# Decode attention with a gated FFN: every large load issued as two halves of 64 partitions, from SyncE's queue and from ScalarE's

## The chip, the core and the metric

The kernel runs on one core of a Trainium2 chip. The metric is the device time of one execution in microseconds. All inputs lie in HBM and have to be brought into SBUF, the on-chip memory with 128 partitions. Five engines work side by side, each through its own queue in program order: TensorE (PE in the profile, PEld for its weight loads), VectorE (DVE), ScalarE (ACT), GpSimd (POOL) and SyncE (SP). DMAs are issued by an engine's queue and carried out by 16 DMA engines, which the profile shows together as DMA.

## The reference

One decode step for a batch of 4 with 32 heads of 128, a cache of 4096 keys and values for each head, and a GEGLU feed-forward layer beside it. All data are float32.

```python
q = (x @ wq).reshape(4, 1, 32, 128).transpose(0, 2, 1, 3)
p = softmax(einsum("bhqd,bhkd->bhqk", q, k_cache) * 128 ** -0.5)
a = einsum("bhqk,bhkd->bhqd", p, v_cache)      # transposed and reshaped to (4, 1, 4096)
a = a @ wo
b = (gelu(x @ w_gate) * (x @ w_up)) @ w_down
g = sigmoid((x * gate_w).sum(-1, keepdims=True))
out = g * a + (1 - g) * b
```

The key cache and the value cache are 268 MB each, so nearly all the bytes are k and v, and each is used once.

## The kernel before

The work is cut into NT = 64 steps. Step i takes two heads (a pair of heads, g = i // 4) of one batch element (b = i % 4). For each step there is one k load and one v load, each a tile `kv` of 128 partitions by 8192 float32 (32 KB in each partition, 4 MB in all): 64 partitions belong to each of the two heads, and a partition holds 64 rows of the cache. The pool `kv` has five such buffers. The query weights wq (two tiles), the FFN's w_gate and w_up (one tile each) and w_down (one tile, filled by four DMAs) pass through the same five buffers.

All loads come from one list, in the order in which they are needed: q0, q1, k0, k1, v0, k2, v1, k3, v2, and so on. The function `load` (L51) issues one entry, and `load_next` takes the next entry of the list. The last v tile, v63, is loaded in two DMAs that split its columns. The output weights wo come in 16 loads of 512 KB into a pool of their own (`load_wo`, L87 to L89), one every four steps, and gate_w in 13 tiny ones (`load_gw`). All DMAs are issued by SyncE.

In the main loop, step i does this, in this program order:

- `scores_a(i)` (L187): VectorE multiplies the last 8 of the 64 cache rows in each partition with the query (tile `pa`).
- `soft_max(i - 1)`: VectorE takes the maximum per head (L214, the second `m`), TensorE spreads it to the partitions (L217), ScalarE scales it (L219, `nb`) and takes the exponentials (L222, `pm`).
- `scores_d(i)`: four times VectorE multiplies 14 rows (L187, `pr`) and sums them (L198); ScalarE sums the 8 rows of `pa` (L200). Then comes one `load_next`.
- `pv(i - 1)` (L247): TensorE multiplies the probabilities with the v tile, in 32 matmuls. Then comes another `load_next`.
- `o_out(i - 1)`: ScalarE copies the result out of PSUM (L254, `o`), TensorE folds it with 8 passes (L258, `oT`).
- `max_a(i)`: VectorE takes the maximum of a partition (L207), TensorE transposes it (L209).

After step 1 the two `load_next` of step i issue v(i+1) and k(i+3). A load into a `kv` buffer has to wait until the buffer's last reader is done: the last product of VectorE for a k tile, the last matmul of `pv` for a v tile. `q_spread` (L175, L178, tile `qb`) prepares the queries of the next pair of heads every four steps, `project_a` and `ffn_down` (both by L240) are the output products, and after step 63 there is one more pass (i = 64) with `pv(63)`, the last projections, and the result's DMA (L363).

The Tile framework adds the waits. It gives every DMA, whichever engine issues it, one of eight completion semaphores in turn. A DMA that is given a semaphore again waits until the DMA that had it before, eight DMAs earlier, has landed. That wait stands on the queue of the issuing engine, ahead of the DMA, and everything behind it on that queue waits too.

Of the kernel before, what the change touches and what calls it, by code (L numbers as in the profile page):

```python
# [17 lines left out]
def tile_gated_mix(ctx: ExitStack, tc: tile.TileContext, x, kc, vc, wq, wo, w_gate, w_up, w_down, gate_w, out):  # L18
    nc = tc.nc
    P = 128  # L20
    B, H, S, D = kc.shape
    DM = x.shape[2]
    F = w_gate.shape[1]
    KC = DM // P
# [6 lines left out]
    TW = R * D  # L31
# [16 lines left out]

    T = {}

    def load(kind, i):  # L51
        t = T[kind, i] = kv.tile([P, TW], F32, name="kv")
        if kind in "kv":
            h, b = HT * (i // B), i % B
            src = (kc if kind == "k" else vc)[b, h:h + HT].rearrange("h (p r) d -> (h p) (r d)", p=PH)
            n = 2 if (kind, i) == ("v", NT - 1) else 1
            for s in range(n):
                nc.sync.dma_start(t[:, s * TW // n:(s + 1) * TW // n], src[:, s * TW // n:(s + 1) * TW // n])  # L58
        elif kind == "q":
            nc.sync.dma_start(t, wq.rearrange("(p c) n -> p (c n)", c=KC)[:, i * TW:(i + 1) * TW])  # L60
        elif kind == "f":
            nc.sync.dma_start(t[:, :KC * F], (w_gate, w_up)[i].rearrange("(p c) n -> p (c n)", c=KC))
        else:
            for f0 in range(0, F, FG):
                f1 = min(f0 + FG, F)
                n = (f1 - f0) // P
                nc.sync.dma_start(t[:, f0 // P * DM:(f0 // P + n) * DM],
                                  w_down[f0:f1].rearrange("(p i) n -> p (i n)", i=n))

    loads = [("q", 0), ("q", 1), ("k", 0)]  # L70
    for i in range(NT):
# [8 lines left out]
    def load_next():  # L80
        n = next(loads, None)
        if n:
            load(*n)
# [302 lines left out]
```

## Time and profile before

| what | value |
|---|---|
| median of 3 runs | 1329.67 us (1329.47 to 1330.52) |
| the profiled execution | 1329.66 us |
| its span, from the first to the last instruction | 1327.9 us |
| TensorE's mean granted clock | 0.653 |
| busy: VectorE, TensorE, ScalarE | 1147.5, 536.3, 325.7 us |
| read from HBM | 564.67 MB, 425 GB/s over the span |
| k loads, v loads: median from issue to landing | 42.6 us, 34.2 us |

The 1.76 us between the profiled execution's own time and its span lie outside of the recorded instructions. An issue-to-landing time is not the time that a transfer needs by itself: it holds the wait behind the transfers that were issued earlier. The share of DMA is counted over all 16 DMA engines.

### The profile page before, as it was taken

What the parts mean: (1) busy time and instruction counts of PE and PEld (TensorE: products, weight loads), DVE (VectorE), ACT (ScalarE), POOL (GpSimd) and SP (SyncE); (2) the same over time, 40 slices, a digit from 0 to 9 for tenths busy, and PEclk for the clock granted to TensorE, in tenths of its full rate; (3) what the DMA queues carried; (4) which work ended last, traced back from release to release, by engine and by line L of the source; (5) the groups of instructions that cost most, each with busy time, mean ns of one, the idle gap of its engine ahead of it and who ended that gap; (6) DMA issues with size and microseconds to landing.
All of it is one profiled execution on the core that took longest, in us unless ns stands there. A gap on an engine that the chain in (4) does not pass through costs nothing.

```text
span 1327.9 us, 10223 instructions
## 1 busy us (share of the span) xinstructions
PE 536.3 (40%) x3690; PEld 191.2 (14%) x3690; DVE 1147.5 (86%) x783; ACT 325.7 (25%) x1435; POOL 0.7 (0%) x6
## 2 busy tenths in 40 slices
PE   3243433443442453443443343343343344343345
PEld 1011111111120121111111111111111111111112
DVE  1999898898898679889889889889889889889885
ACT  0232222223222122312312212212312312212211
POOL 0000000000000000000000000000000000000000
PEclk9656666666666775665666676666666666665677
DMA  9999999999999999999999999999999999999996
GB/s 411 426 425 434 432 427 426 436 427 429 429 433 429 428 430 431 430 430 430 430 429 432 430 427 433 431 429 426 431 433 430 429 427 436 427 427 433 431 428 287
DMA packets 24414, 565.33 MB, mean 426 GB/s; under 512 B 2712, under 2 KB 2728, under 8 KB 6956
## 3 DMA queue, kind: packets, MB, share of 16 engines
q1 hardware_dynamic: 24364, 564.69, 99.3%
q8 instruction: 29, 0.48, 0.1%
q14 instruction: 21, 0.17, 0.0%
HBM read 564.67 MB, written 0.01 MB: 425 GB/s over the span
## 4 chain that ended last, share of the span: by engine, by line
DMA 68%; DVE 26%; PE 4%; issue 1%; SPq 0%; ACT 0%; DVEq 0%; ACTq 0%
DMA kv<-in_A_k_cache 50%; DMA kv<-in_A_v_cache 18%; DVE pr L187 13%; DVE sc L198 11%; PE po L247 4%; DVE pa L187 2%; PE q L289 0%; DVE m L214 0%; PE b_acc L240 0%; SPq L58 0%; DVE m L207 0%; PE oT L258 0%; ACT pm L222 0%; DVE ot L270 0%; SPq L60 0%
## 5 line engine op out<-in xcount | busy, mean ns | idle before, releaser
L247 PE MATMUL po<-kv,pm 128*8 128x512 f32 x2048 | 364.8, 878 | 490.4 <-DMA kv<-in_A_v_cache 488.0
L198 DVE TENSOR_REDUCE sc<-pr 128x14 f32<-128x1792 f32 x256 | 517.1, 2020 | 8.8
L187 DVE TENSOR_TENSOR pr<-kv,qb 128x1792 f32<-128x1792 f32 x256 | 516.9, 2019 | 6.6
L254 ACT ACTIVATE o<-po 128x512 f32<-128x512 f32 x64 | 38.2, 597 | 584.1 <-PE po L247 584.1
L247 PEld LDWEIGHTS po<-kv,pm 128*8 128x8 f32 x2048 | 67.2, 116 | 736.8 <-issue 725.7
L187 DVE TENSOR_TENSOR pa<-kv,qb 128x1024 f32<-128x1024 f32 x64 | 78.4, 1224 | 107.8 <-DMA kv<-in_A_k_cache 107.8
L200 ACT ACTIVATE dump<-pa 128x128 f32<-128x128 f32 x512 | 158.3, 309 | 18.8 <-DVE pa L187 3.2
L200 ACT ACTIVATION_READ_ACCUMULATOR dump<-pa 128x1 f32 x512 | 95.3, 186 | 0.0
L258 PE MATMUL oT<-sel,o 128*128 128x2 f32 x512 | 67.4, 254 | 45.5 <-ACT o L254 45.5
L217 PE MATMUL sm<-m,ones 1*64 1x1 f32 x256 | 23.1, 244 | 154.3 <-DVE m L214 154.3
L219 ACT ACTIVATE nb<-sm 128x1 f32<-128x1 f32 x64 | 11.0, 171 | 295.9 <-PE sm L217 295.8
L258 PEld LDWEIGHTS oT<-sel,o 128*128 128x128 f32 x512 | 61.9, 191 | 107.1 <-ACT o L254 107.1
L209 PE MATMUL sm<-ident,m 128*1 128x128 f32 x64 | 18.6, 290 | 76.1 <-DVE m L207 75.5
L222 ACT ACTIVATE pm<-sc,nb 64x64 f32<-64x64 f32 x128 | 44.9, 351 | 2.8
L217 PEld LDWEIGHTS sm<-m,ones 1*64 1x64 f32 x256 | 17.7, 190 | 170.5 <-DVE m L214 169.3
L222 ACT ACTIVATION_READ_ACCUMULATOR pm<-sc,nb 64x1 f32 x128 | 23.7, 185 | 0.0
L178 ACT ACTIVATE qb<-q 128x512 f32<-128x512 f32 x16 | 9.6, 597 | 51.7 <-PE q L175 51.7
L175 PE MATMUL q<-ident,QT 128*64 128x128 f32 x256 | 20.1, 306 | 0.6 <-DVE QT L162 0.6
L207 DVE TENSOR_REDUCE m<-sc 128x1 f32<-128x64 f32 x64 | 14.1, 220 | 6.6
L214 DVE TENSOR_REDUCE m<-sm 1x2 f32<-1x128 f32 x64 | 17.3, 270 | 0.5 <-PE sm L209 0.5
L240 PE MATMUL a_acc<-wo_sb,ot 128*32 128x128 f32 x256 | 16.9, 412 | 0.0
L209 PEld LDWEIGHTS sm<-ident,m 128*1 128x1 f32 x64 | 5.1, 80 | 79.5 <-issue 38.3
(49 smaller groups left out, 95.0 us busy)
## 6 DMA issues: line engine op xcount, KB each, us to landing
kv<-in_A_k_cache SPq DMA_DIRECT2D x64, 4096.0 KB, 42.6
kv<-in_A_v_cache SPq DMA_DIRECT2D x63, 4096.0 KB, 34.2
kv<-in_A_wq SPq DMA_DIRECT2D x2, 4096.0 KB
wo_sb<-in_A_wo SPq DMA_DIRECT2D x16, 512.0 KB, 43.1
kv<-in_A_v_cache SPq DMA_DIRECT2D x2, 2048.0 KB
kv<-in_B_w_gate SPq DMA_DIRECT2D x1, 3584.0 KB
kv<-in_B_w_up SPq DMA_DIRECT2D x1, 3584.0 KB
kv<-in_B_w_down SPq DMA_DIRECT2D x3, 1024.0 KB, 26.4
```

Of the source, the lines that this page charges most:

```text
L175: nc.tensor.matmul(ps[h * PH:(h + 1) * PH, b, :], QT[:, HT * g + h, b:b + 1].to_broadcast([P, PH]), ident, start=True, stop=True)
L187: nc.vector.tensor_tensor(t, k[:, r0:r1], QB[g][:, b:b + 1, :].to_broadcast([P, r1 - r0, D]), op=OP.mult)
L198: nc.vector.tensor_reduce(SC[i][:, r0:r1], pr, axis=AX.X, op=OP.add)
L200: nc.scalar.activation(dump, PA[i][:, r - A_ROWS[0], :], AF.Copy, accum_out=SC[i][:, r:r + 1])
L209: nc.tensor.transpose(MT[i], m1, ident)
L214: nc.vector.tensor_reduce(m2, MT[i].rearrange("o (h p) -> o h p", h=HT), axis=AX.X, op=OP.max)
L217: nc.tensor.matmul(nbp[h * PH:(h + 1) * PH, :], ones[:1, :PH], m2[:, h:h + 1], start=True, stop=True)
L222: nc.scalar.activation(PM[i % 3][s, :, h], SC[i][s, :], AF.Exp, bias=nb[s, :], scale=scale, accum_out=RS[g % 2][s, b, h:h + 1])
L240: nc.tensor.matmul(acc[32 * c:32 * c + 32, :], t, w[:, c * C4:(c + 1) * C4], start=start, stop=stop)
L247: nc.tensor.matmul(PO[i % 2][32 * c:32 * c + M].rearrange("p j d -> p (j d)"), p[:, j * M:(j + 1) * M], T["v", i][:, j * N:(j + 1) * N], s ...
L254: nc.scalar.activation(o, PO[i % 2], AF.Copy)
L258: nc.tensor.matmul(OT[g][:, b, :], o[:, j, :], sel[:, j, :], start=j == 0, stop=j == RJ - 1)
```

## The change

A helper `rows` issues each large load twice: partitions 0 to 63 from SyncE's queue, partitions 64 to 127 from ScalarE's. It stands in for every `dma_start` in `load`, so for wq, k, v, w_gate, w_up and w_down; the two column halves of v63 and the four parts of w_down are each split in the same way, which makes 137 DMAs into 274. The loads of x, wo and gate_w and the store of the result stay whole on SyncE's queue. Bytes, buffers and arithmetic are the same.

```diff
+    def rows(dst, src):
+        for eng, p in ((nc.sync, 0), (nc.scalar, P // 2)):
+            eng.dma_start(dst[p:p + P // 2], src[p:p + P // 2])
+
     def load(kind, i):
...
             for s in range(n):
-                nc.sync.dma_start(t[:, s * TW // n:(s + 1) * TW // n], src[:, s * TW // n:(s + 1) * TW // n])
+                rows(t[:, s * TW // n:(s + 1) * TW // n], src[:, s * TW // n:(s + 1) * TW // n])
         elif kind == "q":
-            nc.sync.dma_start(t, wq.rearrange("(p c) n -> p (c n)", c=KC)[:, i * TW:(i + 1) * TW])
+            rows(t, wq.rearrange("(p c) n -> p (c n)", c=KC)[:, i * TW:(i + 1) * TW])
         elif kind == "f":
-            nc.sync.dma_start(t[:, :KC * F], (w_gate, w_up)[i].rearrange("(p c) n -> p (c n)", c=KC))
+            rows(t[:, :KC * F], (w_gate, w_up)[i].rearrange("(p c) n -> p (c n)", c=KC))
         else:
...
-                nc.sync.dma_start(t[:, f0 // P * DM:(f0 // P + n) * DM],
-                                  w_down[f0:f1].rearrange("(p i) n -> p (i n)", i=n))
+                rows(t[:, f0 // P * DM:(f0 // P + n) * DM], w_down[f0:f1].rearrange("(p i) n -> p (i n)", i=n))
```

In the program as built, ScalarE's queue has in step i, in this order: the 8 sums of `pa` (L200 of before), ScalarE's half of v(i+1), its half of k(i+3), then the copy `o` of step i - 1. In step 62 the four halves of w_down stand there, ahead of the copy `o` of step 61. With twice the DMAs in the same eight semaphores, the DMA eight before is only about two steps back: k(i+3) waits for a half of k(i+1) in most steps, and the last part of w_down waits for the second column half of v63.

## The prediction

> **What bounds the kernel now.** I read the page from the top: the busy row, the slices of DMA, the DMA queues, and the chain that ended last.
>
> ```profile
> PE 536.3 (40%) x3690; PEld 191.2 (14%) x3690; DVE 1147.5 (86%) x783; ACT 325.7 (25%) x1435; POOL 0.7 (0%) x6
> ...
> DMA  9999999999999999999999999999999999999996
> GB/s 411 426 425 434 432 427 426 436 427 429 429 433 429 428 430 431 430 430 430 430 429 432 430 427 433 431 429 426 431 433 430 429 427 436 427 427 433 431 428 287
> DMA packets 24414, 565.33 MB, mean 426 GB/s; under 512 B 2712, under 2 KB 2728, under 8 KB 6956
> ...
> q1 hardware_dynamic: 24364, 564.69, 99.3%
> ...
> DMA 68%; DVE 26%; PE 4%; issue 1%; SPq 0%; ACT 0%; DVEq 0%; ACTq 0%
> ```
>
> The DMA engines are full from end to end, at one rate. Nearly all bytes come through one queue (q1, SyncE's). VectorE at 86% is second. The windows view gives start, middle and end, and the waits of VectorE say how much slack it has:
>
> ```profile
> core 0: us, PE busy (x) PEld busy (x) DVE busy (x) ACT busy (x) POOL busy (x), PEclk, DMA share, GB/s
> 0.00:10.00 10.00, 0.00 (x0) 0.00 (x0) 0.82 (x7) 1.28 (x1) 0.70 (x6) 1.00 0.89 354
> 300.00:1250.00 950.00, 387.43 (x2584) 136.17 (x2584) 839.21 (x559) 238.31 (x1054) 0.00 (x0) 0.64 1.00 430
> 1290.00:1328.00 38.00, 19.21 (x228) 9.36 (x228) 21.38 (x19) 7.10 (x29) 0.00 (x0) 0.78 0.73 305
> ```
> ```profile
> DVE pa L187 <- DMA kv<-in_A_k_cache: 107.8, 57, 10.9
> ```
>
> In the middle the rate is 430 GB/s at a DMA share of 1.00, so a 4.19 MB load takes 4.19 / 0.430 = 9.75 us and a step (k and v) 19.5 us. VectorE waits 57 times for a k tile, 107.8 / 57 = 1.9 us each: that is its slack in a step. The other rows of the DMA view of the same stretch say how deep the queue is:
>
> ```profile
> q1 hardware_dynamic: 16982, 407.85, 100.2%
> ...
> kv<-in_A_v_cache SPq DMA_DIRECT2D x47, 4096.0 KB, 34.2
> kv<-in_A_k_cache SPq DMA_DIRECT2D x46, 4096.0 KB, 43.1
> ```
>
> A load lands 34 to 43 us after its issue and needs 9.75, so some 24 us or more of work lie ahead of each load. A load that is issued up to 24 us late starves nothing.
>
> **The change part by part.**
>
> *Bytes and packets.* The bytes stay. 137 DMAs more are issued. Each is closed by small completion packets: of the 2712 packets under 512 B, 128 are the rows of gate_w, and the other 2584 are 16 for each of the 153 DMAs over 128 partitions and one per partition of the narrow ones (128 for gate_w, 4 each for x and the result). If a half leaves 16 too, that is 137 x 16 = 2192 more, 137 for each DMA engine. A window of 17 ns that holds one such packet prices it:
>
> ```profile
> q1 hardware_dynamic: 1, 0.00, 3.3%
> ```
>
> 3.3% of 16 engines x 17 ns is 9 ns; 137 x 9 ns = **+1.2 us**.
>
> *The rate.* No row shows two queues that both carry large loads. The ends: nothing, or what an engine loses when another queue comes between. The second has rows: two windows in which one 32 KB packet of q1 starts, right behind an instruction fetch of q14 on the same engine (0.10 us wide, from 524.12; 0.06 us wide, from 484.52):
>
> ```profile
> q1 hardware_dynamic: 1, 0.03, 99.6%
> ```
> ```profile
> q1 hardware_dynamic: 1, 0.03, 195.3%
> ```
>
> 99.6% of 16 x 0.10 us is 1.59 us, 195.3% of 16 x 0.06 is 1.87 us; undisturbed, 407.85 MB took 100.2% of 16 x 950 us, which is 37.3 us for a MB and 1.22 us for 32 KB. So a return from a fetch costs 0.37 to 0.65 us. I take nothing for the rate: a fetch goes to another place than SBUF and may just be slow to write, while two load queues have the same source and target. The other end is a rival below.
>
> *ScalarE's queue.* It gets 137 issues at 0.33 us (the L58 rows below), 45 us beside 325.7 busy: hidden by its idle time, as long as no wait of theirs holds back what is behind. Such a wait is new in each step. One step of before:
>
> ```profile
> 593.12 0.33 SPq L58 DMA_DIRECT2D kv<-in_A_v_cache  x1
> ...
> 593.15 0.60 ACT L254 ACTIVATE o<-po 128x512 f32<-128x512 f32 x1 [9.31 <-PE po L247]
> 593.54 0.38 SPq L58 DMA_DIRECT2D kv<-in_A_k_cache  x1
> 593.80 1.05 PE L258 MATMUL oT<-sel,o 128*128 128x2 f32 x8 [0.72 <-ACT o L254]
> 595.25 0.22 DVE L207 TENSOR_REDUCE m<-sc 128x1 f32<-128x64 f32 x1
> 595.61 0.37 PE L209 MATMUL sm<-ident,m 128*1 128x128 f32 x1 [0.75 <-DVE m L207]
> 596.85 1.23 DVE L187 TENSOR_TENSOR pa<-kv,qb 128x1024 f32<-128x1024 f32 x1 [1.38 <-DMA kv<-in_A_k_cache]
> 597.99 0.27 DVE L214 TENSOR_REDUCE m<-sm 1x2 f32<-1x128 f32 x1
> ```
>
> Both loads of the step are issued at 593, when their buffers come free. With the eight semaphores, k(i+3) now also waits for k(i+1), which lands at 596.8. Behind it on ScalarE stands the copy `o`, then on TensorE `oT` and the transpose (L209), then VectorE's maximum (L214). From the landing: issue 0.33, `o` 0.60, `oT` 1.05, transpose 0.37 and the gaps of these rows make about 2.5 us, where VectorE gets to L214 after 1.14. So it stands still for 1.3 us, and the 1.9 us of slack hide it; without that cover it would be 63 x 1.3 = 82 us. The loads themselves go out 3.5 us late, out of 24.
>
> *The start.* ScalarE's half of v1 waits for k1, and `qb` (L178) is behind it:
>
> ```profile
> 29.88 0.60 ACT L178 ACTIVATE qb<-q 128x512 f32<-128x512 f32 x1 [2.90 <-PE q L175]
> ...
> 32.37 1.23 DVE L187 TENSOR_TENSOR pa<-kv,qb 128x1024 f32<-128x1024 f32 x1 [3.77 <-DMA kv<-in_A_k_cache]
> ```
>
> k1 is the fourth load, so it lands one load after k0: VectorE begins about 10 us late. The queue's 24 us hide this, and VectorE makes it up in some 5 to 8 steps; without cover it is 10 us.
>
> *The end.* Here nothing hides a delay: everything after the last k tile is a chain.
>
> ```profile
> 1250.11 44.21 DMA kv<-in_A_k_cache
> ...
> 1324.89 0.35 DVE res L362
> ```
> ```profile
> 1289.94 1.75 SPq L67 DMA_DIRECT2D kv<-in_B_w_down  x4
> ...
> 1290.07 0.60 ACT L254 ACTIVATE o<-po 128x512 f32<-128x512 f32 x1 [9.41 <-PE po L247]
> ...
> 1295.48 0.27 DVE L214 TENSOR_REDUCE m<-sm 1x2 f32<-1x128 f32 x1
> ...
> 1304.20 5.76 PE L247 MATMUL po<-kv,pm 128*8 128x512 f32 x32 [8.02 <-DMA kv<-in_A_v_cache]
> ```
>
> k63 lands at 1294.3, and the span ends 33.6 us later, without another wait for a load. Now ScalarE's part of w_down comes ahead of `o` of step 61, and its last DMA waits for the second half of v63. v62 lands at 1304.2, v63 takes 9.75 more. If the two queues run level, ScalarE is thus stuck until about 1313.9; `o` and the chain above let L214 start at about 1316.3 where it started at 1295.5, and all four products of step 63 are behind it on VectorE: **+20.8 us**. If ScalarE's queue is ahead by a time x, the wait is shorter by x, but then those halves of v62 and v63 went in front of SyncE's half of k63, which lands x later. The end thus moves by the larger of x and 20.8 - x. x is at most the two halves, 2 x 2.10 MB / 0.430 = 9.75 us. So this costs 11 to 21 us, wherever the queues stand. The wo loads bear on that:
>
> ```profile
> wo_sb<-in_A_wo SPq DMA_DIRECT2D x16, 512.0 KB, 43.1
> ```
>
> 16 x 0.52 = 8.4 MB are on SyncE's queue alone, twice the 4.2 MB of these two halves; if the engines serve the queues evenly, ScalarE's is ahead by the most it can be well before the end. I take **+14 us**, nearer to 11. [...]
>
> *Sum.* 1329.66 (profiled execution; the median is 0.01 us off) + 1.2 + 14 = **1345 us**, and by the two ends of the last part 1342 to 1352.
>
> **The rivals.**
>
> *A queue change costs time on every packet.* If an engine alternates and each 32 KB packet takes 1.59 us in place of 1.22, a factor of 1.30, the time up to k63's landing less the wo loads (1294.3 - 8.4 / 0.430 = 1274.8 us) grows to 1660; with 19.5 for wo, 33.6 and 1.8 outside that is 1715 us, and with 1.87 us (factor 1.53) about 2005. For: it is the only row with a change of queue. Against: it is a fetch.
>
> *The halves stand in each other's way.* If 64 partitions can be written at only half the rate of 128, because all 16 engines then write into one half of SBUF, two queues help only while some engines write the lower half and others the upper. If all are always in the same half, everything but wo takes twice as long: 2 x 1274.8 + 19.5 + 35.4 = 2605 us. If they meet half of the time, 1.5 times: 1967. For: 1.22 us a packet in every engine at once looks like a hard limit, and no row says whether it is the engine's or the memory's. Against: no row shows a slower load of 64 partitions; every large load has 128. [...]
>
> *Not slower.* Two queues fill what one leaves empty. The place is the whole middle: 430 GB/s there, 436 in the best slice of the page. At 436, 1274.8 us shrink by 1.4%, 17.5 us, and the start (354 GB/s in the first 10 us) could give 1.8 us. That gives 1326 to 1328 us. It decides from a middle rate of 435, where the gain reaches the 15 us of the sum. Against: the DMA share is 1.00 already.
>
> *The change is not what it says*: ScalarE might issue its halves so late that they follow SyncE's one by one. Its issues lag by 3.5 us of 24, so it isn't likely and has no chance of its own.
>
> **How the numbers follow.** Forecast (rate kept, 11 to 21 us at the end) 0.52, its own range 1338 to 1353. Halves in each other's way 0.24, spread over 1400 to 2605, half of it under 1967. A change of queue costs 0.12 (1400 to 2005). Not slower 0.12: 0.05 of it faster by over 0.2% (below 1327), 0.07 within 0.2% (1327 to 1332.3), where a part of the end's cost is won back. 0.2% is about what a measurement of this kernel can tell from no change. From 1327 up to 2000 leaves out 0.05 below and 0.12 above, so that is the range. Faster 0.05, same 0.07, slower 0.88.
>
> **What would show it.** Right: a middle rate of 430 with q1 and a second queue at equal bytes (less wo); 4904 packets under 512 B; `pa` waiting for k while L214 waits 1.3 us a step for L209; in the last 60 us either k63 landing up to 10 us late, or L214 of step 62 standing up to 21 us behind ScalarE. Wrong: a middle rate below 425 with DMA share still 1.00 is one of the first two rivals, and there every step's k wait grows; if VectorE has no waits for k left, the 1.3 us weren't hidden. If the end after the last k is still 33.6 us and the middle 430, the term of 14 us falls.

## The result, and the profile after

The changed kernel takes **2529.94 us** (median of 6 runs, 2514.71 to 2540.62), the kernel before 1330.21 us beside it (6 runs, 1329.47 to 1330.99): **1.901 times as long** (95% interval 1.898 to 1.9045). The forecast was 1345 us with a range of 1327 to 2000. It was wrong by nearly a factor of two, and the time lies beyond the range.

The page of the changed kernel (its lines are four lower than before: L54 is the helper's DMA, L191 the products, L202 the sums, L213 the transpose, L218 the maximum `m`, L251 `pv`, L258 the copy `o`, L262 `oT`):

```profile
PE 586.9 (23%) x3690; PEld 235.6 (9%) x3690; DVE 1151.2 (45%) x783; ACT 324.8 (13%) x1435; POOL 0.7 (0%) x6
...
DMA  9999999999999999999999999999999999999996
GB/s 211 212 215 217 224 224 219 222 228 223 238 234 236 223 236 252 219 227 225 222 234 215 230 221 225 232 215 225 216 229 225 218 226 217 232 231 224 232 219 165
DMA packets 26608, 565.36 MB, mean 223 GB/s; under 512 B 4904, under 2 KB 4920, under 8 KB 9148
...
q1 hardware_dynamic: 15596, 286.55, 51.0%
q10 hardware_dynamic: 10960, 278.14, 48.5%
...
L191 DVE TENSOR_TENSOR pa<-kv,qb 128x1024 f32<-128x1024 f32 x64 | 78.4, 1225 | 1084.9 <-DMA kv<-in_A_k_cache 1062.3
```

The busy times of VectorE (1147.5 us before, 1151.2 now) and ScalarE hardly moved, and the bytes are the same. The DMA row is full of nines in both pages: the DMA engines are as "busy" as before and move half as much. Here a share of 1.00 says that each engine has a packet under way, not that bytes flow (1.00 at 430 GB/s before, 1.01 at 228 GB/s now, from 300 to 1250 us); only the GB/s row tells the two apart. The time went into VectorE's waits for k, 1062.3 us where 107.8 were. The two queues carry the bytes that were predicted for them: 286.55 and 278.14 MB differ by 8.4 MB, which is wo.

The middle of the run (windows view: PE, PEld, DVE, ACT, POOL busy, clock, DMA share, GB/s), and the DMA view of the same stretch:

```profile
300.00:1250.00 950.00, 231.00 (x1407) 94.02 (x1411) 449.83 (x302) 127.97 (x565) 0.00 (x0) 0.57 1.01 228
```
```profile
DMA packets 10024, 216.90 MB, mean 228 GB/s; under 512 B 1920, under 2 KB 1920, under 8 KB 3456
q1 hardware_dynamic: 5930, 110.20, 51.6%
q10 hardware_dynamic: 4073, 106.43, 48.8%
```

228 GB/s where 430 were. 216.90 MB took 100.4% of 16 x 950 us: 70.4 us for a MB, **2.31 us for a packet of 32 KB**, where it was 1.22. The next question is whether this is the change of queue or the half. One stretch has hardly any change of queue (1990 to 1996 us; packets that start in it, MB, and their time as a share of 16 engines times 6 us):

```profile
q1 hardware_dynamic: 44, 1.05, 83.4%
q10 hardware_dynamic: 5, 0.16, 12.0%
```

1.05 MB are 32 packets of 32 KB; 83.4% of 96 us is 80 us, 2.5 us for each. Nearly all packets come from one queue here, and they are as slow. And near the start the two queues can be seen taking turns. Four windows of 1.2 or 1.3 us, in order (from 16.2, 18.6, 21.0 and 23.5 us); no packet starts between these windows:

```profile
q1 hardware_dynamic: 16, 0.52, 200.4%
...
q1 hardware_dynamic: 16, 0.52, 213.9%
q10 hardware_dynamic: 16, 0.00, 1.6%
...
q10 hardware_dynamic: 16, 0.52, 184.9%
...
q10 hardware_dynamic: 16, 0.52, 214.0%
q1 hardware_dynamic: 16, 0.00, 1.5%
```

In each window 16 packets of 32 KB start, one for each DMA engine, and all 16 come from one queue: **all engines write the lower half, or all write the upper one**, 2.4 us at a time (200.4% of 16 x 1.2 us, over 16 packets). The other half is idle meanwhile. In the second and the fourth window there are 16 small packets of the other queue besides (1.6% and 1.5%), each just ahead of a large one. So here the packets of the two queues alternate, and large ones behind a small one of the other queue took 2.57 us each (213.9% and 214.0% of 16 x 1.2 us), those behind a large one of the other queue 2.40 (the third window, 184.9% of 16 x 1.3 us). As all of them stand behind a packet of the other queue, these windows don't price a change of queue.

That all engines are in one half is true of the start, and it isn't the whole loss. Later in the run packets of both queues start side by side (from 1001 to 1002 us, 8 of q1 and 2 of q10), but in the page's slices the rate stays between 211 and 252 GB/s to the last but one. The start and the length of each packet in the trace tell how many of the 32 KB packets under way belong to each half. Between 300 and 1250 us a packet with 15 or more in its own half, itself included, took 2.52 us on average. One with 6 to 9 there, so that both halves were written about evenly, still took 2.12 us, far from 1.22.

The end, too, is longer. The first product of the last k tile (step 63):

```profile
2478.99 1.23 DVE L191 TENSOR_TENSOR pa<-kv,qb 128x1024 f32<-128x1024 f32 x1 [12.01 <-DMA kv<-in_A_k_cache]
```

From there to the end of the span (2530.8 us) it is 51.8 us, where it was 33.6. Up to there it is 2479.0 us, where it was 1294.3.

### The profile page after: what moved, and what is told of

The parts are those of the page before. It is cut to its first block, busy times and chain, and to the rows that moved or that the text cites. A ratio compares the mean times of both kernels' runs of the same rounds, so it can differ in the third digit from the quotient of the medians.

```text
span 2530.8 us, 10566 instructions
## 1 busy us (share of the span) xinstructions
PE 586.9 (23%) x3690; PEld 235.6 (9%) x3690; DVE 1151.2 (45%) x783; ACT 324.8 (13%) x1435; POOL 0.7 (0%) x6
## 2 busy tenths in 40 slices
DMA packets 26608, 565.36 MB, mean 223 GB/s; under 512 B 4904, under 2 KB 4920, under 8 KB 9148
## 3 DMA queue, kind: packets, MB, share of 16 engines
q1 hardware_dynamic: 15596, 286.55, 51.0%
q10 hardware_dynamic: 10960, 278.14, 48.5%
## 4 chain that ended last, share of the span: by engine, by line
another core or an unknown queue 56%; DVE 22%; PE 10%; DMA 6%; issue 2%; ACT 2%; ACTq 1%; SPq 0%; DVEq 0%
DVE sc L202 10%; DVE pr L191 10%; PE po L251 6%; DMA kv<-in_A_v_cache 4%; PE oT L262 2%; DMA kv<-in_A_wq 2%; DVE pa L191 1%; ACTq L54 1%; ACT o L258 1%; ACT dump L204 1%; DVE m L218 1%; PE sm L221 0%; ACT pm L226 0%; PE sm L233 0%
## 5 line engine op out<-in xcount | busy, mean ns | idle before, releaser
L251 PE MATMUL po<-kv,pm 128*8 128x512 f32 x2048 | 366.1, 880 | 975.9 <-DMA kv<-in_A_v_cache 817.1
L191 DVE TENSOR_TENSOR pa<-kv,qb 128x1024 f32<-128x1024 f32 x64 | 78.4, 1225 | 1084.9 <-DMA kv<-in_A_k_cache 1062.3
L202 DVE TENSOR_REDUCE sc<-pr 128x14 f32<-128x1792 f32 x256 | 517.1, 2020 | 8.8
L191 DVE TENSOR_TENSOR pr<-kv,qb 128x1792 f32<-128x1792 f32 x256 | 516.9, 2019 | 6.6
L262 PE MATMUL oT<-sel,o 128*128 128x2 f32 x512 | 104.5, 326 | 663.4 <-ACT o L258 663.4
L258 ACT ACTIVATE o<-po 128x512 f32<-128x512 f32 x64 | 38.2, 597 | 1687.0 <-DMA kv<-in_A_k_cache 613.8
L251 PEld LDWEIGHTS po<-kv,pm 128*8 128x8 f32 x2048 | 66.8, 116 | 1223.4 <-issue 1220.9
L262 PEld LDWEIGHTS oT<-sel,o 128*128 128x128 f32 x512 | 99.0, 288 | 725.4 <-ACT o L258 725.4
L218 DVE TENSOR_REDUCE m<-sm 1x2 f32<-1x128 f32 x64 | 17.5, 273 | 85.7 <-PE sm L213 85.7
L221 PEld LDWEIGHTS sm<-m,ones 1*64 1x64 f32 x256 | 18.6, 200 | 225.7 <-DVE m L218 222.1
L213 PE MATMUL sm<-ident,m 128*1 128x128 f32 x64 | 22.6, 353 | 46.4 <-DVE m L211 46.4
L179 PE MATMUL q<-ident,QT 128*64 128x128 f32 x256 | 28.1, 388 | 0.6 <-DVE QT L166 0.6
L179 PEld LDWEIGHTS q<-ident,QT 128*64 128x64 f32 x256 | 22.3, 201 | 3.9 <-issue 2.7
```

The source lines that it names most:

```text
L179: nc.tensor.matmul(ps[h * PH:(h + 1) * PH, b, :], QT[:, HT * g + h, b:b + 1].to_broadcast([P, PH]), ident, start=True, stop=True)
L191: nc.vector.tensor_tensor(t, k[:, r0:r1], QB[g][:, b:b + 1, :].to_broadcast([P, r1 - r0, D]), op=OP.mult)
L202: nc.vector.tensor_reduce(SC[i][:, r0:r1], pr, axis=AX.X, op=OP.add)
L213: nc.tensor.transpose(MT[i], m1, ident)
L218: nc.vector.tensor_reduce(m2, MT[i].rearrange("o (h p) -> o h p", h=HT), axis=AX.X, op=OP.max)
L221: nc.tensor.matmul(nbp[h * PH:(h + 1) * PH, :], ones[:1, :PH], m2[:, h:h + 1], start=True, stop=True)
```

## The experiments

The theory after this result is the rival of the prediction, **the halves**: 64 neighbouring partitions can be written at half the rate, whatever queue they come from. Its rivals are **the queues** (an engine that goes back and forth between two queues of large loads pays at each packet) and **the count** (a DMA of fewer partitions is slow as such). A second group of runs asks where the forecast's 15 us would have been right. All edits are to the helper `rows` of the changed kernel unless said otherwise; `...` in a diff marks lines left out. Times of the kernel before on the same chips were 1330.4 to 1330.7 us.

### Both halves on one queue

```diff
-        for eng, p in ((nc.sync, 0), (nc.scalar, P // 2)):
-            eng.dma_start(dst[p:p + P // 2], src[p:p + P // 2])
+        for p in (0, P // 2):
+            nc.sync.dma_start(dst[p:p + P // 2], src[p:p + P // 2])
```

> Both halves of 64 partitions are issued by SyncE, lower half first; ScalarE issues none. Theory H (all 16 engines write into one half of the partitions at a time, and a half takes only half the rate): still about 225 GB/s and 2500 us, a 32 KB packet at about 2.35 us. Theory Q (each change between two queues costs an engine about 1.1 us a packet): no change of queue is left, so 430 GB/s and about 1330 to 1345 us. Theory W (loads held back by waits on ScalarE's queue): about 1330 us too.

Measured: **2532.98 us** (one run). The page's rate and queue, and the middle:

```profile
GB/s 207 207 208 212 209 209 210 210 207 210 212 208 214 211 211 215 211 212 213 210 212 212 211 212 210 215 216 221 219 217 230 235 230 239 241 277 273 331 343 183
...
q1 hardware_dynamic: 26556, 564.70, 99.7%
```
```profile
300.00:1250.00 950.00, 192.71 (x1281) 66.84 (x1281) 404.65 (x273) 113.22 (x498) 0.00 (x0) 0.58 1.01 211
```

No second queue, and the same time as with two (2514.71 to 2540.62). The price is the halves', not the queues'. The way there differs a little: in the middle two queues move 228 GB/s and one 211, 7% less, which the one queue makes up at the end of the run (up to 343 GB/s).

### Two queues, whole loads: v from ScalarE, the rest from SyncE

```diff
-    def rows(dst, src):
-        for eng, p in ((nc.sync, 0), (nc.scalar, P // 2)):
-            eng.dma_start(dst[p:p + P // 2], src[p:p + P // 2])
+    def rows(dst, src, kind=None):
+        (nc.scalar if kind == "v" else nc.sync).dma_start(dst, src)
...
-                rows(t[:, s * TW // n:(s + 1) * TW // n], src[:, s * TW // n:(s + 1) * TW // n])
+                rows(t[:, s * TW // n:(s + 1) * TW // n], src[:, s * TW // n:(s + 1) * TW // n], kind)
```

> Whole loads of 128 partitions, v tiles from ScalarE's queue and all others from SyncE's, so both queues carry large loads at the same time. H: the full rate of 430 GB/s, 1330 to 1360 us, packets of 1.22 us. Q: engines still change queue after each packet, so some 2.3 us a packet and about 2500 us.

Measured: **1345.46 us** (4 runs, 1344.14 to 1346.76; ratio 1.0114, interval 1.0098 to 1.0129). Its middle:

```profile
300.00:1250.00 950.00, 396.15 (x2579) 141.93 (x2571) 836.59 (x558) 236.70 (x1047) 0.00 (x0) 0.64 1.00 430
```

430 GB/s with 296.25 MB on one queue and 268.44 MB on the other: two queues of large loads cost nothing per packet. The queues fall as a cause of the lost rate. The 15 us that are left aren't rate either: the product `pa` of step 63 starts at 1308.08 us, 13.7 us later than before, as in the odd-even runs below.

### Two queues, halves by columns

```diff
-        for eng, p in ((nc.sync, 0), (nc.scalar, P // 2)):
-            eng.dma_start(dst[p:p + P // 2], src[p:p + P // 2])
+        n = dst.shape[-1] // 2
+        for eng, c in ((nc.sync, 0), (nc.scalar, n)):
+            eng.dma_start(dst[:, c:c + n], src[:, c:c + n])
```

> The same split in two, the same two queues, issues and waits as in the changed kernel, but cut by columns: each half has all 128 partitions and 16 KB rows. H: the full rate, and what is left is the cost at the end that was forecast, 11 to 21 us: 1342 to 1352 us. Q: twice as many packets, each with the same loss of 1.1 us: 3500 us or more. W: as slow as the changed kernel, about 2530 us.

Measured: **1362.58 us** (4 runs, 1362.39 to 1363.13; ratio 1.0243, interval 1.0226 to 1.0261).

```profile
300.00:1250.00 950.00, 429.44 (x2601) 173.30 (x2601) 833.73 (x560) 237.24 (x1054) 0.00 (x0) 0.63 1.01 426
```

With 128 partitions in each half the rate is back at 426. The time misses the 1342 to 1352 us that were expected. The run has 44144 packets, as each row is cut in two; 426 in place of 430 GB/s are some 12 of the 32 us (an estimate: 1274.8 us of loads, stretched by 430/426), and the rest wasn't taken apart. It is a loss of another order than the 1200 in question.

### Two queues, odd and even partitions

```diff
-        for eng, p in ((nc.sync, 0), (nc.scalar, P // 2)):
-            eng.dma_start(dst[p:p + P // 2], src[p:p + P // 2])
+        for eng, p in ((nc.sync, 0), (nc.scalar, 1)):
+            eng.dma_start(dst[p::2], src[p::2])
```

> 64 partitions for each queue as in the changed kernel, but the even ones from SyncE and the odd ones from ScalarE, so that each DMA reaches both halves of the partitions. H, if it is the place of the partitions that counts: faster than the changed kernel, from 1345 us (full rate) up to about 1900 if engines still meet now and then. If any DMA of 64 partitions is slow, or Q: about 2530 us again.

Measured: **1351.73 us** (one run), with the same number of partitions, packets and bytes in each DMA as in the changed kernel:

```profile
300.00:1250.00 950.00, 430.86 (x2612) 172.66 (x2612) 842.69 (x566) 238.91 (x1062) 0.00 (x0) 0.63 1.00 429
```

So 64 partitions are not too few. **Which** 64 they are decides: 228 GB/s for neighbours, 429 for every second one.

In this edit, and in the next ones, a partition's place in SBUF and its address in HBM change together, so the source could be the reason. wq speaks against that. Its rows of 32 KB lie 64 KB apart in HBM, just as the odd rows of a k tile do, but they go to neighbouring partitions. The four windows of 16 to 25 us above are from the wq loads, with 2.4 to 2.6 us for a packet; the odd rows of k took 1.22 us (429 GB/s).

### Smaller pieces: neighbours against partitions spread out

Four runs from SyncE's queue alone, one each, with the place of the partitions and their number moved apart:

```diff
-        for eng, p in ((nc.sync, 0), (nc.scalar, P // 2)):
-            eng.dma_start(dst[p:p + P // 2], src[p:p + P // 2])
+        for p in range(0, P, P // 4):
+            nc.sync.dma_start(dst[p:p + P // 4], src[p:p + P // 4])
...
+        for p in range(4):
+            nc.sync.dma_start(dst[p::4], src[p::4])
...
+        for p in range(0, P, P // 8):
+            nc.sync.dma_start(dst[p:p + P // 8], src[p:p + P // 8])
...
+        for p in range(8):
+            nc.sync.dma_start(dst[p::8], src[p::8])
```

Each run has one of the four loops. Quarters in a row, the first:

> Each large load in four DMAs of 32 neighbouring partitions, all from SyncE's queue. [...] If the rate goes with the number of partitions in the DMA, it halves once more: about 107 GB/s, 5000 us.

Every fourth partition:

> Each large load in four DMAs of 32 partitions, every fourth partition, all from SyncE's queue. If the place of the partitions counts and not their number, the rate is 430 GB/s, and the time that of the kernel before plus three times the completion packets of one more split, 1330.7 + 3 x 1.2 = 1334 us, up to 1345 if the shorter queue (eight DMAs are now two tiles) starves the DMA engines at times. If the number of partitions counts, 2500 to 5000 us.

Eighths in a row:

> Each large load in eight DMAs of 16 neighbouring partitions, all from SyncE's queue. [...] If the limit is one for a whole half of SBUF, 16 partitions are as good as 64 and it stays near 2530 to 2600 us.

Every eighth partition:

> Each large load in eight DMAs of 16 partitions, every eighth partition, so that both halves of SBUF are always written. [...] If only it matters that both halves are written, or that neighbours are avoided, it is 1335 to 1345 us.

The middle of the four runs, in this order:

```profile
300.00:1250.00 950.00, 193.95 (x1281) 66.89 (x1281) 403.10 (x272) 113.21 (x498) 0.00 (x0) 0.57 1.01 212
```
```profile
300.00:1250.00 950.00, 385.52 (x2575) 134.93 (x2579) 838.08 (x560) 237.71 (x1053) 0.00 (x0) 0.64 1.01 430
```
```profile
300.00:1250.00 950.00, 107.16 (x730) 37.13 (x730) 243.36 (x161) 65.56 (x290) 0.00 (x0) 0.54 1.01 125
```
```profile
300.00:1250.00 950.00, 191.61 (x1283) 66.63 (x1283) 404.82 (x278) 113.23 (x498) 0.00 (x0) 0.57 1.01 213
```

| partitions in one DMA | GB/s, 300 to 1250 us | time |
|---|---|---|
| 32, neighbours | 212 | 2585.25 us |
| 32, every fourth | 430 | 1332.94 us |
| 16, neighbours | 125 | 3551.75 us |
| 16, every eighth | 213 | 2691.15 us |

The count falls: 32 spread out (430 GB/s, 1332.94 us where 1334 was expected) are twice as fast as 64 in a row (211), and 32 in a row (212) as fast as those, where the count would have halved the rate. One limit for a whole half falls too: 16 in a row got 125 GB/s and 3551.75 us and not 2530 to 2600. It isn't "both halves at once" either: every eighth partition always writes both halves and gets 213 GB/s, half the rate, so the 1335 to 1345 us fall. What is measured is that the rate goes with which partitions a DMA writes; what makes these groups of partitions differ isn't in the trace and wasn't shown. Nor is the rate of 16 neighbours fixed: it was 114 to 125 GB/s in the first quarter of the run and 206 between 3000 and 3400 us. It climbs while the run goes on, as it does for halves on one queue (207 to 343).

### Eight engines out of step, one queue

This run and the next try a theory of the author's: the rate is lost because the engines are in step and all write the same half at a time, as in the four windows above. The base is the kernel with both halves on SyncE's queue; in `load`, the second wq tile comes otherwise:

```diff
+        elif (kind, i) == ("q", 1):
+            s1 = wq.rearrange("(p c) n -> p (c n)", c=KC)[:, TW:2 * TW]
+            for p in range(4):
+                nc.sync.dma_start(t[p:32:4], s1[p:32:4])
+            nc.sync.dma_start(t[32:], s1[32:])
         elif kind == "q":
```

> Lower half and upper half, both from SyncE's queue, as in the run that took 2533 us, with one change at the start: the lower 32 partitions of the second wq tile come in four DMAs of 8 partitions, every fourth partition, so that, if such a DMA is carried out by only 8 of the 16 DMA engines, those 8 fall four packets behind the others once. [...] If halves are bound to be written one after the other whatever the engines do, the rate stays at 211 GB/s and the time at 2530 us. [...]

Measured: **2534.47 us** (one run). Two windows of 10 us, behind the shift, and the middle:

```profile
20.00:30.00 10.00, 6.12 (x32) 1.93 (x36) 0.88 (x4) 0.00 (x0) 0.00 (x0) 1.00 1.00 260
30.00:40.00 10.00, 0.79 (x8) 0.00 (x0) 0.00 (x0) 0.00 (x0) 0.00 (x0) 0.67 0.98 167
...
300.00:1250.00 950.00, 189.88 (x1242) 65.85 (x1242) 399.49 (x271) 114.09 (x505) 0.00 (x0) 0.57 1.01 208
```

260 GB/s for a moment, then 167, and 208 in the middle. The four DMAs of 8 partitions left 8 small packets each and not 16 (an estimate from the pages: 4920 packets under 512 B, where both halves on one queue had 4904), which fits 8 engines for each. No lasting gain came. But the shift didn't last either: by the packets in the trace, those that start between 20 and 50 us took from 1.3 to 4.2 us, and then they come again in the rhythm of the run without a shift, most of them at 2.3 to 2.6 us. What a lasting shift would do isn't shown.

### Eight engines out of step, two queues

The base is the changed kernel, with one small load more among the first ones:

```diff
-    for _ in range(NB - 2):
-        load_next()
+    load_next()
+    load_next()
+    spare = consts.tile([8, KC], F32)
+    nc.sync.dma_start(spare, gate_w.rearrange("(p c) -> p c", c=KC)[:8])
+    load_next()
```

> The changed kernel (lower half from SyncE, upper half from ScalarE), with one small load more at the start on SyncE's queue: 8 rows of gate_w into a spare tile that nothing reads. In the changed kernel's records each DMA engine takes a packet from one queue and then one from the other, and at first all 16 write the same half at once. If the small load gives 8 of the engines one packet more on SyncE's queue, these write the upper half while the other 8 write the lower one. If being in step is what keeps the two queues from adding up, packets take 1.2 us in place of 2.4 from about 40 us on and the rate goes to 350 to 430 GB/s for as long as the shift lasts: with the rest of the run as it was, 1400 to 2300 us. [...]

Measured: **2522.20 us** (one run), within the range of the changed kernel, and the same rates in the first slices of its page:

```profile
GB/s 211 211 211 224 225 230 235 241 228 234 231 221 230 230 230 232 218 231 226 223 250 212 230 218 226 228 217 231 218 226 224 221 238 214 240 229 226 232 217 156
```

No effect, and no shift either: as in the changed kernel, all of the 16 packets that start from 16.0, and from 18.4 us, are q1's, and all from 20.9, and from 23.4 us, q10's. So this run doesn't test the theory. The step of the engines is seen in the records but not shown as the reason why two queues do not fill both halves. Which engine writes which partition at a time isn't in the trace, so that stays open. That they don't fill them is measured: 2530 us with two queues, 2533 with one. Between 300 and 1250 us, 228 GB/s with two queues are 8% over the 211 with one. Over the whole run nothing of it is left.

### Odd and even partitions on one queue

```diff
-        for eng, p in ((nc.sync, 0), (nc.scalar, P // 2)):
-            eng.dma_start(dst[p:p + P // 2], src[p:p + P // 2])
+        for eng, p in ((nc.sync, 0), (nc.sync, 1)):
+            eng.dma_start(dst[p::2], src[p::2])
```

> Odd and even partitions again, both DMAs from SyncE's queue; ScalarE issues nothing. If all that is lost with odd-even halves comes from waits on ScalarE's queue, only the completion packets are left: 1330.7 + 1.2 = 1332 us, within 0.3%. If 64 partitions with gaps are themselves slower to write, or twice the DMAs on eight semaphores delay SyncE's issues too, it stays near 1345 to 1352 us.

Measured: **1331.57 us** (10 runs, 1330.53 to 1332.08; ratio 1.0009, interval 0.9999 to 1.0018). The 1.2 us between the medians (1331.57 less 1330.41) are the forecast's term for completion packets, but the interval runs from nothing to 2.4 us. The trace is sharper: the packets under 512 B took 2.76 us of each DMA engine, where it was 1.53. And all that the odd-even run on two queues lost beyond it, 20 us, comes with the second queue.

### w_down whole from SyncE

Odd and even on two queues as above, and in `load`:

```diff
-                rows(t[:, f0 // P * DM:(f0 // P + n) * DM], w_down[f0:f1].rearrange("(p i) n -> p (i n)", i=n))
+                nc.sync.dma_start(t[:, f0 // P * DM:(f0 // P + n) * DM], w_down[f0:f1].rearrange("(p i) n -> p (i n)", i=n))
```

> The two halves are the odd and the even partitions, as in the run that took 1351.7 us, but the four DMAs of w_down stay whole on SyncE's queue, so that no wait for the last load stands on ScalarE's queue ahead of the copy o of step 61. If the end term of the prediction is right (11 to 21 us, of which ScalarE's wait for v63 was seen with 16.7 us), the time falls by about that much, to 1335 to 1342 us, and VectorE's wait of 8.3 us for the transpose in the last 60 us goes. If the 21 us that the odd-even halves cost lie in the middle, in ScalarE's waits step by step, the time stays at 1348 to 1352 us.

Measured: **1345.86 us** (4 runs, 1344.21 to 1346.46; ratio 1.0116, interval 1.0101 to 1.0131): 5.9 us less, not 10 to 17. The end of the odd-even run before this edit, and of this one:

```profile
1297.85 16.71 ACTq L54 DMA_DIRECT2D kv<-in_B_w_down  x4
...
1307.91 1.22 DVE L191 TENSOR_TENSOR pa<-kv,qb 128x1024 f32<-128x1024 f32 x1
...
1314.61 0.60 ACT L258 ACTIVATE o<-po 128x512 f32<-128x512 f32 x1 [18.34 <-DMA kv<-in_B_w_down]
...
1317.40 0.28 DVE L218 TENSOR_REDUCE m<-sm 1x2 f32<-1x128 f32 x1 [8.28 <-PE sm L213]
```
```profile
1307.94 1.22 DVE L191 TENSOR_TENSOR pa<-kv,qb 128x1024 f32<-128x1024 f32 x1
1309.08 0.27 DVE L218 TENSOR_REDUCE m<-sm 1x2 f32<-1x128 f32 x1
```

The wait that the prediction named is there: w_down's halves hold ScalarE's queue for 16.71 us, `o` comes at 1314.61 and VectorE stands still for 8.28 us at L218. Without it L218 follows at 1309.08. But step 63 starts at 1307.9 in both, 13.6 us after the 1294.34 of the kernel before. The page's issue rows of the first of these runs (KB each, median us from issue to landing) show what is late:

```profile
kv<-in_A_k_cache ACTq DMA_DIRECT2D x64, 2048.0 KB, 21.5
kv<-in_A_k_cache SPq DMA_DIRECT2D x64, 2048.0 KB, 32.6
```

ScalarE's half of a k tile lands after 21.5 us, SyncE's after 32.6. The tile is whole only with the second, 11 us later, and it was moved at the full rate all the same. Most pairs are issued together, but not all. SyncE's queue waits after each wo load but one for that load's semaphore, which its next half of a k tile has been given. These waits, in the same run (us in total, times, longest):

```profile
SPq L54 <- DMA wo_sb<-in_A_wo: 259.1, 15, 20.8
```

In the second half of the run SyncE's half of k is thus issued 14 to 16 us after ScalarE's, once in four steps.

### The first eight loads whole, and wo halved too

Two edits to the run with w_down whole: the first eight large loads stay whole on SyncE's queue (so VectorE starts in time); or the wo loads go odd and even from both queues as well (so the queues carry equal bytes).

```diff
+    first = iter(range(8))
     def rows(dst, src):
+        if next(first, None) is not None:
+            nc.sync.dma_start(dst, src)
+            return
```
```diff
-        nc.sync.dma_start(WO[g], wo[g * HT * D:(g + 1) * HT * D, :].rearrange("(h p) n -> p h n", p=P))
+        rows(WO[g], wo[g * HT * D:(g + 1) * HT * D, :].rearrange("(h p) n -> p h n", p=P))
```

> As the odd-even run with w_down whole (1345.9 us), but the first eight large loads stay whole on SyncE's queue, so that VectorE's first product starts at 32.4 us as before and not at 44.8 us. In that run the product pa of each step was 9 to 13 us later than before from the first step to step 62. If that is the late start carried to the end (ScalarE's waits leave VectorE no slack to make it up), pa of step 63 comes 10 to 12 us earlier and the time falls to 1334 to 1337 us. If the lateness comes from ScalarE's waits in the steps themselves, it builds up again within some ten steps and the time stays at 1342 to 1346 us.

> As the odd-even run with w_down whole (1345.9 us), but the wo loads go half from each queue as well, so that both queues carry the same bytes. If ScalarE's queue gets ahead because the wo loads lie on SyncE's alone, k62 and k63 land in time again (the product pa of step 63 at about 1296 us, where it was at 1307.9) and the time falls by 10 to 13 us, to 1333 to 1336 us. If the queues drift apart by their own waits, pa of step 63 stays near 1308 us and the time at 1343 to 1347 us.

First eight whole: **1343.91 us** (4 runs, 1343.59 to 1344.21; ratio 1.0103, interval 1.0085 to 1.0121). From its timeline the products `pa` of steps 0, 3 and 63 and, between the first two, the last whole load, k3, and ScalarE's halves of v2 and k4:

```profile
32.42 1.23 DVE L196 TENSOR_TENSOR pa<-kv,qb 128x1024 f32<-128x1024 f32 x1 [3.78 <-DMA kv<-in_A_k_cache]
...
47.95 0.33 SPq L56 DMA_DIRECT2D kv<-in_A_k_cache  x1
...
58.20 0.57 ACTq L59 DMA_DIRECT2D kv<-in_A_v_cache  x1
...
65.92 0.50 ACTq L59 DMA_DIRECT2D kv<-in_A_k_cache  x1
...
93.22 1.23 DVE L196 TENSOR_TENSOR pa<-kv,qb 128x1024 f32<-128x1024 f32 x1 [6.99 <-DMA kv<-in_A_k_cache]
...
1307.32 1.22 DVE L196 TENSOR_TENSOR pa<-kv,qb 128x1024 f32<-128x1024 f32 x1
```

The two steps to compare, in the kernel before:

```profile
86.09 1.22 DVE L187 TENSOR_TENSOR pa<-kv,qb 128x1024 f32<-128x1024 f32 x1
...
1294.34 1.23 DVE L187 TENSOR_TENSOR pa<-kv,qb 128x1024 f32<-128x1024 f32 x1 [2.06 <-DMA kv<-in_A_k_cache]
```

VectorE starts in time, but in step 3 it waits 7 us for a tile that is still loaded whole, and is 7.1 us late; at the end it is 13 us late. The late start isn't what is carried to the end. The DMA view from 70 to 80 us says what k3 waited for:

```profile
q1 hardware_dynamic: 65, 2.13, 49.7%
q10 hardware_dynamic: 79, 2.06, 48.0%
```

ScalarE's queue was empty when its halves of v2 and k4 were issued, 10 and 18 us after k3. They got half of the DMA engines' time, while k3 stood in SyncE's queue behind what had been issued before it. **The second queue let loads that are needed later go ahead of a load that is needed now**, at the full rate (429 GB/s from 50 to 100 us).

wo halved too: **1339.44 us** (4 runs, 1338.81 to 1341.18; ratio 1.0071, interval 1.0053 to 1.0089), 6.4 us less.

```profile
1302.52 1.23 DVE L191 TENSOR_TENSOR pa<-kv,qb 128x1024 f32<-128x1024 f32 x1
```

The time lies between the two that were expected. Step 63 comes 8.2 us late and no longer 13.6. So wo on SyncE's queue alone makes about two fifths of the lateness. Whether by its bytes or by the wait for its semaphore isn't parted, as this edit takes both away; what keeps ScalarE's queue ahead for the rest wasn't tried.

## Why the prediction was wrong, point by point

- **The rate** is the step that failed: "I take nothing for the rate ... two load queues have the same source and target." It left open which part of the target a load reaches, and that was the trouble. And where an instruction fetch is written, on which it argued, no row shows. In its place stands a factor. In the middle the rate is 228 GB/s and not 430, 1.89 times less. Over all the loads, 2479.0 us less 19.5 for wo is 2459.5 us where 1274.8 were, 1.93 times. It isn't the second queue, of which that paragraph thought alone (two queues of whole loads kept 430 GB/s), but the 64 neighbouring partitions (one queue of halves fell to 211).
- **The halves in each other's way** is the rival that came true in its size, near its end for engines that are always in the same half (2605 us, reckoned with 215 GB/s where the page has 223 on the mean, and without the 18 us by which the end grew). Its picture was too simple: it has two queues add up whenever some engines write the lower half and others the upper, and in the middle packets took 2.12 us even then. Why is open. The rival had 0.24, and the range cut its upper half off. Against it stood that no row shows a slower load of 64 partitions. But no row could: every large load before had 128. The absence of a row isn't evidence against, and a range that is to hold the bounds of an unknown cost has to reach to its end.
- **A change of queue** (0.12, priced at 1715 to 2005 us) is refuted by the run with whole loads on two queues.
- **Completion packets**: 4904 predicted, 4904 on the page; 1.2 us predicted, and with odd and even on one queue the packets under 512 B took 1.23 us more of each DMA engine.
- **ScalarE's queue** was put at 1.3 us of standing still in each step, hidden by the waits for k. The odd-even run on two queues, where the rate is kept, shows another pattern (VectorE's waits: us in total, times, longest). VectorE stands still at L218 in 17 steps, and only 11 steps wait for k, where 57 did. It is late itself and finds its k tile there in most steps, so little is left of the slack that was to hide such delays.

```profile
DVE m L218 <- PE sm L213: 47.2, 17, 8.3
DVE pa L191 <- DMA kv<-in_A_k_cache: 40.1, 11, 4.8
```

- **The start** was right for the delay and wrong for its cover: with odd and even partitions VectorE began at 42.3 us and not at 32.4 (the row below), which it was to make up in 5 to 8 steps, and it was never back in time: the product `pa` of every later step is at least 9 us late. That isn't the start carried on (the run with the first eight whole shows this): a tile is whole only with SyncE's half, 11 us after ScalarE's. The prediction had this time, as x in the last term, but counted it for the end alone and took 9.75 us for its most.

```profile
42.26 1.23 DVE L191 TENSOR_TENSOR pa<-kv,qb 128x1024 f32<-128x1024 f32 x1 [9.60 <-ACT qb L182]
```

- **The end**: "the larger of x and 20.8 - x" should have been nearer to a sum. With the rate kept, L218 of step 62 came 21.9 us late (1317.40 against 1295.48): 13.6 us for the late k tile and 8.3 us behind w_down. So 1351.73 us lies within the 1338 to 1353 of the forecast's own range, but partly by luck: the route was only half understood. In the changed kernel itself, where the last loads move at half the rate too, the end grew by 18 us (51.8 less 33.6).

## What to carry to other kernels

Here a load's rate went with which partitions it writes, not with the number of queues or DMAs: 430 GB/s for all 128, 429 and 430 for every second and every fourth, 211 to 213 for 64 or 32 neighbours and for every eighth on one queue (228 for 64 neighbours from two), 125 for 16 neighbours. So in a case like this one keep 128 partitions in a load, or cut by a stride of two or four and not by halves. And where all DMA engines are busy already, ask of a second queue what it could fill: here the best split (odd and even, one queue) came out even, and every spread over two queues that kept the full rate cost 9 to 32 us. In the odd-even runs that is because one queue runs ahead and the order in which the loads are needed is lost.

## What the runs showed of the hardware that was not expected

- 32 spread partitions in a DMA reach the rate of 128: 430 GB/s in pieces of every fourth partition, 1332.94 us.
- Pieces of neighbours on one queue speed up by themselves in a long run: from 207 to 343 GB/s for halves, from 118 to 210 for eighths. Pieces with every eighth partition do not (204 to 216). This looks like engines that slowly get out of step, but it isn't shown: in the two runs that were to put them out of step the shift was lost again by 50 us, or never came.
- An engine busy for 100% of the time tells nothing of bytes: the DMA share was 1.00 or 1.01 at 125, 212, 228 and 430 GB/s alike.
